# Every second column of a head per product, w_in loaded in column halves, v loaded in head halves

## The chip, the core and the metric

The kernel runs on one core of a Trainium2 chip. Its time is what one execution takes on the device, in microseconds. The times below are medians of several executions; beside them stands one execution taken by the hardware profiler, from which all lines of the profile come. In these lines PE is TensorE's matrix multiplication, PEld its weight load, DVE is VectorE, ACT is ScalarE, POOL is GpSimd, and SP is SyncE, which here only issues DMAs. A q behind an engine (POOLq, SPq) is its queue of instructions.

## What is computed

Attention with a forget gate, for 8 batches of 8 heads with 576 positions and a head width of 64, then a two-layer network with gelu over all heads together (4608 rows of 512, hidden width 2048):

```python
scores = scale * np.matmul(q, k.transpose(0, 1, 3, 2))
cum = np.cumsum(np.log(np.clip(f, 0.0001, 1.0)), axis=-1)
decay = cum[:, :, :, None] - cum[:, :, None, :]
scores = np.where(causal, -1000000000.0, scores + decay)
attn = softmax(scores)                         # cut: max, exp, sum
attn_out = np.matmul(attn, v)
x = attn_out.transpose(0, 2, 1, 3).reshape(B * S, H * D)
out = gelu_tanh(x @ w_in) @ w_out
```

## The kernel before

**Quads.** The heads are worked four at a time. Quad i holds four heads of batch i//2, so there are 16 quads and two of them make the 512 columns of x for one batch. For a quad, q and k are loaded by GpSimd's queue with a cast to bf16 (`load_qk`, L94) and transposed by VectorE (`transpose_qk`, L120). The decay is split: exp(−cum − 64) of a key's position, `wT`, is multiplied into v (`make_vw`, L129), so a product with the exponentials of the scores carries it; the factor of the query's position cancels when the product is divided by the denominator, which is the product of the same exponentials with `w_bf`, the bf16 copy of `wT`.

**Rounds.** A quad's scores are computed in three rounds (`score_round`, L139), each of which fills two pairs of PSUM banks; ScalarE writes their exponentials into the strips of `pt` (L166), and GpSimd sets what lies above the diagonal to zero (`mask(i, r)`, L169): two instructions for round 0, one for round 1, two for round 2.

**Products.** `product` (L186) adds six parts, the slots in `product_parts` (L183): the first four need the masks of rounds 0 and 1, the last two that of round 2. `denominators(i)` (L226) does it with `w_bf` into the bank pair "po", and VectorE turns the result into reciprocals spread over the partitions (`reciprocals`, L213: a transpose, L215, a reciprocal, L217, and a transpose back, L219). `attn_out(i, y)` (L229) does it with half y of the head's columns of `vw`, and `normalise` (L223) multiplies with the reciprocals and writes `xT[:, 2*(i%2)+y, :]`: 32 columns of four heads on 128 partitions. The pool of "po" has one buffer, so the next user of it waits until VectorE has read the last.

**The network.** `w_in_sb` (128, 4, 2048) holds w_in in the order of these partitions: for slab dt = 2u+y the rows of half u, column half y of each head. `mlp_in(b, fts)` (L249) goes over blocks of 128 hidden columns, four slabs each, and ScalarE applies gelu (L245). `mlp_out` (L260) multiplies with `w_out`; in the later steps its matmuls are dealt out between the rounds of the next quads (`step`, `pull`).

**Order.** Everything runs in the order in which it is written, on each engine (`manual_schedule`). Dependencies between instructions and the waits for them are worked out by the framework. GpSimd's queue carries all loads with a cast, the masks and, from quad 2 on, make_vw; so whatever is issued there stands ahead of what comes later.

**The start.** `startup` (L294) is written out by hand for quads 0 and 1. GpSimd issues q and k of quads 0 and 1, fills the unused part of `v_nat` with zeros (L299), issues the five loads of v for batch 0 (L102, one for each tile of 128 positions, all 8 heads in it) and slab 0 of w_in (L112); then come the masks of quad 0 with slabs 1 to 3 of w_in between them, the masks of quad 1, the q and k of quad 2 between mask(1,1) and mask(1,2), and the four loads of w_out (L116). VectorE does the scan of log f, the transposes of q and k, and make_vw(0) and make_vw(1). TensorE's order is: three score rounds of quad 0 and two of quad 1 with matmuls on a blank tile (`warm_up`, L290) between them, `denominators(0)`, the last score round of quad 1, `attn_out(0, 0)`, `attn_out(0, 1)`, then for quad 1 the first four parts of the denominators and of the product, their last two parts, the second product, and the first two column blocks of the network.

These are the two lines on which the order of w_in and of v rests:

```python
w_in_hbm = moe_w_in.rearrange("(u g y i) n -> u y g i n", u=QPB, g=4, y=2)
in_=v[b, :, s0:s0 + 128 - r, :].rearrange("h p d -> p h d")
```

Of the kernel before, what the change touches and what calls it, by code (L numbers as in the profile page):

```python
# [16 lines left out]
def kernel(  # L17
# [10 lines left out]
    nc = tc.nc  # L28

    B, H, S, D = q.shape  # L30
    BH = B * H
    NT = (S + 127) // 128
    LAST = S - 128 * (NT - 1)
    scale = 1.0 / (D ** 0.5)

    D_MODEL, D_FF = moe_w_in.shape
# [3 lines left out]
    QPB = H // 4  # L40
# [6 lines left out]
    TAIL, HEAD = NT - 1, NT  # L47
# [14 lines left out]
    def many(n, shape, dtype, name):  # L62
        return [singles.tile(shape, dtype, name=f"{name}{i}") for i in range(n)]
# [6 lines left out]
    v_nat = many(2, [128, NT, H, D], FP32, "v_nat")  # L70
# [3 lines left out]
    vw = many(2, [128, NT + 1, 4, D], BF16, "vw")  # L74
# [3 lines left out]
    w_in_sb = singles.tile([128, N_DT, D_FF], BF16, name="w_in_sb")  # L78
# [3 lines left out]
    wT = singles.tile([128, NQ, NT, 4], FP32, name="wT")  # L82
# [11 lines left out]
    def load_qk(i):  # L94
        b, h0 = i // QPB, 4 * (i % QPB)
        return [nc.gpsimd.dma_start(  # L96
            out=dst[i % 2].rearrange("p a d -> p (a d)"),
            in_=src[b, h0:h0 + 4].rearrange("h (p a) d -> (h p) (a d)", p=32))
            for src, dst in ((k, k_c), (q, q_c))]

    def load_v(b, eng=nc.sync):
        return [eng.dma_start(  # L102
            out=v_nat[b % 2][r:, t, :, :],
            in_=v[b, :, s0:s0 + 128 - r, :].rearrange("h p d -> p h d"),
        ) for t, r, s0 in [(t, 0, 128 * t) for t in range(TAIL)] + [(TAIL, 128 - LAST, S - LAST)]]


    w_in_hbm = moe_w_in.rearrange("(u g y i) n -> u y g i n", u=QPB, g=4, y=2)
    w_out_hbm = moe_w_out.rearrange("(t p) n -> p t n", p=128)

    def load_w_in(dt):
        nc.gpsimd.dma_start(out=w_in_sb[:, dt, :], in_=w_in_hbm[dt // 2, dt % 2])  # L112

    def load_w_out(c):
        n = N_FT // 4
        return nc.gpsimd.dma_start(out=w_out_sb[:, n * c:n * (c + 1), :],  # L116
                            in_=w_out_hbm[:, n * c:n * (c + 1), :])


    def transpose_qk(i):  # L120
        for src, dst in ((k_c, kT), (q_c, qT)):
            nc.vector.transpose(  # L122
                out=dst[i % 2].rearrange("p s c -> p (s c)").bitcast(FP32)
                    .rearrange("p (t a) -> p a t", a=S // 32),
                in_=src[i % 2].rearrange("p a d -> p (a d)").bitcast(FP32)
                    .rearrange("p (a d) -> p a d", d=D // 2),
            )

    def make_vw(i, eng=nc.gpsimd):  # L129
        h0 = 4 * (i % QPB)  # L130
        for p, n, slot in ((128, NT, 0), (64, 1, HEAD)):
            eng.tensor_mul(  # L132
                vw[i % 2][:p, slot:slot + n], v_nat[(i // QPB) % 2][:p, 0:n, h0:h0 + 4, :],
                wT[:p, i, 0:n, :].unsqueeze(3).to_broadcast([p, n, 4, D]))

    def bank_pair(tag, name):
        return pools[tag].tile([128, 2, 512], FP32, name=name, tag=tag)

    def score_round(i, r, tags=("s", "s")):  # L139
        off, parts = rounds[r]  # L140
        n = sum(x[2] for x in parts)
        tiles = [bank_pair(x, "ps_s") for x in tags]
        kk, qq, p = kT[i % 2], qT[i % 2], pt[i % 2]
        def block(c, m0, m, k0, q0, nq, c0, fresh):
            for h in range(4):
                nc.tensor.matmul(  # L146
                    tiles[h // 2][m0:m0 + m, h % 2, c0:c0 + nq],
                    kk[32 * h:32 * h + 32, k0:k0 + m, c],
                    qq[32 * h:32 * h + 32, q0:q0 + nq, c],
                    start=(c == 0 and fresh), stop=(c == 1),  # L150
                    skip_group_check=True,
                )

        if r == 0:
            for c in range(2):
                block(c, 0, 64, 0, 0, 512, 0, True)
                block(c, 64, 64, 64, 64, 448, 64, True)
                block(c, 64, 64, S - LAST, S - LAST, LAST, 0, False)
        else:
            c0 = 0  # L160
            for (t, q0, nq) in parts:
                for c in range(2):
                    block(c, 0, 128, 128 * t, q0, nq, c0, c0 == 0)
                c0 += nq
        for g in range(2):
            nc.scalar.activation(p[:, 2 * g:2 * g + 2, off:off + n],  # L166
                                 tiles[g][:, :, 0:n], AF.Exp, scale=scale)
# [58 lines left out]
    def denominators(i):  # L226
        reciprocals(i, product(i, den_groups(i), bank_pair("po", "po")))

    def attn_out(i, y, tag="po"):  # L229
        normalise(i, y, product(i, out_groups(i, y), bank_pair(tag, "po")))  # L230
# [52 lines left out]
    def make_w(cum):  # L283
        for (r, t0, t1) in ((0, 0, TAIL), (128 - LAST, TAIL, NT)):
            nc.scalar.activation(
                wT[r:, :, t0:t1, :].rearrange("p i t h -> p t i h"),
                cum[r:, t0 * BH:t1 * BH].rearrange("p (t i h) -> p t i h", i=NQ, h=4),
                AF.Exp, scale=-1.0, bias=shift[r:, :])

    def warm_up(ps, n):  # L290
        for _ in range(n):
            nc.tensor.matmul(ps[:, 0, :], blank[:, 0:128], blank, start=True, stop=True)  # L292

    def startup():  # L294
        nc.sync.dma_start(out=f_sb, in_=f.rearrange("b h s -> (b h) s"))
        load_qk(0)
        make_identity(nc, ident_f32)
        for t_ in v_nat:
            nc.gpsimd.memset(t_[:128 - LAST, TAIL, :, :], 0.0)  # L299
        load_qk(1)  # L300
        load_v(0, nc.gpsimd)
        load_w_in(0)

        nc.vector.memset(blank, 0.0)  # L304
        warm = bank_pair("po", "warm")
        warm_up(warm, 11)
        nc.vector.memset(ones_f32, 1.0)
        nc.vector.memset(shift, -64.0)
        nc.vector.memset(wT[:128 - LAST, :, TAIL, :], 0.0)
        nc.vector.memset(w_bf[LAST:, :, HEAD, :], 0.0)  # L310
        for t_ in vw:
            nc.vector.memset(t_[LAST:, HEAD, :, :], 0.0)
        nc.vector.tensor_scalar(f_sb, f_sb, 1e-4, 1.0, op0=ALU.max, op1=ALU.min)
        nc.scalar.activation(f_sb, f_sb, AF.Ln)
        nc.vector.tensor_tensor_scan(cum_sb, ones_f32, f_sb, 0.0, op0=ALU.mult, op1=ALU.add)
        cum = bank_pair("x", "small")[:, 0, 0:NT * BH]
        for t in range(NT):
            s0 = min(128 * t, S - 128)
            nc.tensor.transpose(cum[:, t * BH:(t + 1) * BH],
                                cum_sb[:, s0:s0 + 128], ident_f32)  # L320
        make_w(cum)
        warm_up(warm, 6)
        transpose_qk(0)
        transpose_qk(1)
        nc.vector.tensor_copy(w_bf[:, :, :NT, :], wT)
        nc.vector.tensor_copy(w_bf[:LAST, :, HEAD, :], wT[:LAST, :, 0, :])
        make_vw(0, nc.vector)
        make_vw(1, nc.vector)

        for r, tags in enumerate((("s", "s"), ("x", "s"), ("s", "x"))):  # L330
            score_round(0, r, tags)
            warm_up(warm, 5)
            mask(0, r)
            load_w_in(r + 1)
        score_round(1, 0)
        warm_up(warm, 5)
        score_round(1, 1, ("x", "s"))
        denominators(0)
        mask(1, 0)
        score_round(1, 2, ("s", "x"))  # L340
        attn_out(0, 0)
        mask(1, 1)
        load_qk(2)
        attn_out(0, 1, "s")
        mask(1, 2)
        for c in range(4):
            load_w_out(c)
        first, rest = slice(0, 4), slice(4, 6)
        pod, po0, po1 = (bank_pair(x, "po") for x in ("s", "po", "x"))
        product(1, den_groups(1), pod, first)  # L350
        product(1, out_groups(1, 0), po0, first)
        reciprocals(1, product(1, den_groups(1), pod, rest))
        r0 = product(1, out_groups(1, 0), po0, rest)
        r1 = product(1, out_groups(1, 1), po1)
        ph0, ph1 = (bank_pair("s", "ps_h") for _ in range(2))
        mlp_mm(0, 0, ph0, (0, 1))
        normalise(1, 0, r0)
        normalise(1, 1, r1)
        mlp_mm(0, 1, ph1, (0, 1))
        for dt in (2, 3):  # L360
            mlp_mm(0, 0, ph0, (dt,))
            mlp_mm(0, 1, ph1, (dt,))
        gelu(0, 0, ph0)
        gelu(0, 1, ph1)
        load_qk(3)
        after(load_v(2)[0], load_v(1, nc.gpsimd)[-1])
# [39 lines left out]
    with tc.manual_schedule():  # L406
# [5 lines left out]
        for b in range(B):  # L412
# [18 lines left out]
            elif b + 1 < B:  # L431
                i = 2 * b + 3
# [36 lines left out]
```

## Time and profile before

| | us |
|---|---|
| median of 3 executions (351.93 to 352.19) | 352.18 |
| the profiled execution | 351.2 |
| its span, first to last instruction | 349.5 |
| TensorE busy in it | 334.8 |

The mean granted clock of TensorE over the span is 0.989 of full speed. The span begins with the first instruction; the profiled execution has 1.7 us around it. The views used below are: the chain of work that ended last, in order of time (start, length, engine, tile and line, count); the timeline (start, length, engine, line, operation, output and inputs, count, and in brackets the idle time before it with what ended it); windows (for a stretch of time: its length, busy time and count of each engine in the order PE, PEld, DVE, ACT, POOL, then the granted clock, the share of the DMA engines' time and GB/s); groups by line (busy time, mean ns of one, idle time before them); and issues of DMAs (count, KB as written, median us from issue to landing).

### The profile page before, as it was taken

What the parts mean: (1) busy time and instruction counts of PE and PEld (TensorE: products, weight loads), DVE (VectorE), ACT (ScalarE), POOL (GpSimd) and SP (SyncE); (2) the same over time, 40 slices, a digit from 0 to 9 for tenths busy, and PEclk for the clock granted to TensorE, in tenths of its full rate; (3) what the DMA queues carried; (4) which work ended last, traced back from release to release, by engine and by line L of the source; (5) the groups of instructions that cost most, each with busy time, mean ns of one, the idle gap of its engine ahead of it and who ended that gap; (6) DMA issues with size and microseconds to landing.
All of it is one profiled execution on the core that took longest, in us unless ns stands there. A gap on an engine that the chain in (4) does not pass through costs nothing.

```text
span 349.5 us, 10980 instructions
## 1 busy us (share of the span) xinstructions
PE 334.8 (96%) x5022; PEld 197.5 (57%) x5022; DVE 122.1 (35%) x163; ACT 198.1 (57%) x244; POOL 125.6 (36%) x166
## 2 busy tenths in 40 slices
PE   6938999999999999999999999999999999999995
PEld 2425754467544774457544675457644675557642
DVE  6477032743244503424234422425143312430021
ACT  4851666776655566656745567565664566515400
POOL 8784219765143242625044251624026400300000
PEclk9978999999999999999999999999999999999999
DMA  7999998349510490109511292117301000010021
GB/s 133 190 181 188 218 197 203 64 80 231 100 64 34 118 209 7 62 33 199 103 57 42 69 212 53 35 62 168 68 34 62 33 32 2 33 64 30 2 86 64
DMA packets 43007, 33.37 MB, mean 95 GB/s; under 512 B 31056, under 2 KB 33104, under 8 KB 42960
## 3 DMA queue, kind: packets, MB, share of 16 engines
q0 software_dynamic: 9568, 16.00, 25.8%
q1 hardware_dynamic: 33392, 16.67, 17.3%
q8 instruction: 39, 0.64, 0.8%
q14 instruction: 8, 0.07, 0.1%
HBM read 36.85 MB, written 9.44 MB: 132 GB/s over the span
## 4 chain that ended last, share of the span: by engine, by line
PE 86%; ACT 3%; DMA 3%; DVE 2%; issue 2%; POOL 2%; ACTq 0%; DVEq 0%; POOLq 0%
PE ps_h L236 36%; PE pso L268 32%; PE po L193 10%; PE ps_s L146 8%; DMA v_nat<-in_v_dram 3%; ACT pt L166 3%; DVE vw L132 1%; POOL v_nat L102 1%; DVE den L215 0%; POOL q_c L96 0%; POOL k_c L96 0%; POOL v_nat L299 0%; DVE rb L219 0%; DVE xT L224 0%; DVE o_st L273 0%
## 5 line engine op out<-in xcount | busy, mean ns | idle before, releaser
L268 PE MATMUL pso<-w_out_sb,gT 128*32 128x512 bf16 (+1 forms) x1908 | 134.6, 379 | 0.0
L236 PE MATMUL ps_h<-xT,w_in_sb 128*128 128x288 bf16 x1024 | 128.6, 286 | 1.2 <-ACT gT L245 0.5
L245 ACT ACTIVATE gT<-ps_h 128x576 bf16<-128x576 f32 x128 | 82.3, 650 | 72.3 <-PE ps_h L236 72.3
L166 ACT ACTIVATE pt<-ps_s 128x1024 bf16<-128x1024 f32 x96 | 92.5, 1025 | 48.6 <-PE ps_s L146 47.8
L236 PEld LDWEIGHTS <-w_in_sb 128*128 128x128 bf16 x1024 | 99.3, 98 | 31.5 <-issue 4.7
L177 POOL TENSOR_SCALAR_AFFINE_SELECT pt<-pt 128x512 bf16<-128x512 bf16 (+1 forms) x80 | 52.1, 659 | 130.7 <-ACT pt L166 129.4
L268 PEld LDWEIGHTS <-gT 128*32 128x32 bf16 (+1 forms) x1908 | 59.1, 97 | 53.2 <-issue 0.8
L273 DVE COPY o_st<-pso 128x512 f32<-128x512 f32 x36 | 24.7, 685 | 70.3 <-PE pso L268 70.2
L215 DVE STREAM_TRANSPOSE den<-po 128x576 f32<-128x576 f32 x16 | 12.5, 782 | 83.7 <-PE po L193 83.7
L132 POOL TENSOR_TENSOR vw<-v_nat,wT 128x1280 bf16<-128x1280 f32 (+1 forms) x28 | 40.6, 1472 | 0.2
L224 DVE TENSOR_TENSOR xT<-po,rb 128x576 bf16<-128x576 f32 x32 | 24.1, 757 | 46.3 <-PE po L193 46.2
L146 PE MATMUL ps_s<-qT,kT 32*64 32x64 bf16 (+6 forms) x896 | 36.2, 293 | 1.6 <-ACT pt L166 0.7
L193 PE MATMUL po<-pt,vw 128*32 128x64 bf16 (+4 forms) x768 | 29.1, 289 | 5.3 <-DVE den L215 5.3
L146 PEld LDWEIGHTS <-kT 32*128 32x128 bf16 (+1 forms) x896 | 15.3, 98 | 27.4 <-issue 24.0
L193 PEld LDWEIGHTS <-vw 128*32 128x32 bf16 x768 | 13.9, 100 | 20.0 <-issue 11.2
L122 DVE STREAM_TRANSPOSE kT<-k_c 128x576 f32<-128x576 f32 x16 | 19.9, 1245 | 12.4 <-DMA k_c<-in_k_dram 12.4
L122 DVE STREAM_TRANSPOSE qT<-q_c 128x576 f32<-128x576 f32 x16 | 19.9, 1243 | 1.3 <-DMA q_c<-in_q_dram 1.1
L96 POOL DMA_DIRECT2D k_c<-in_k_dram x16 | 9.1, 572 | 29.2 <-DVE kT L122 24.8
L193 PE MATMUL po<-pt,w_bf 128*32 128x512 bf16 (+5 forms) x384 | 14.7, 285 | 0.0
L219 DVE STREAM_TRANSPOSE rb<-rec 128x576 f32<-128x576 f32 x16 | 12.4, 778 | 0.5
L166 ACT ACT_TABLE_LOAD x7 | 9.0, 1283 | 5.9 <-PE ps_s L146 5.9
L292 PE MATMUL warm<-blank 128*128 128x512 bf16 x37 | 10.4, 427 | 1.3 <-DVE blank L304 1.3
(32 smaller groups left out, 62.9 us busy)
## 6 DMA issues: line engine op xcount, KB each, us to landing
out_dram<-o_st SPq DMA_DIRECT2D x36, 256.0 KB, 2.0
v_nat<-in_v_dram SPq DMA_DIRECT2D x24, 256.0 KB, 6.2
k_c<-in_k_dram POOLq DMA_DIRECT2D x16, 288.0 KB, 6.0
q_c<-in_q_dram POOLq DMA_DIRECT2D x16, 288.0 KB, 7.0
v_nat<-in_v_dram POOLq DMA_DIRECT2D x8, 256.0 KB, 10.8
w_in_sb<-in_moe_w_in_dram POOLq DMA_DIRECT2D x4, 512.0 KB, 16.3
w_out_sb<-in_moe_w_out_dram POOLq DMA_DIRECT2D x4, 512.0 KB, 14.2
v_nat<-in_v_dram SPq DMA_DIRECT2D x6, 128.0 KB, 8.8
```

The source lines that it names most:

```text
L122: nc.vector.transpose(out=dst[i % 2].rearrange("p s c -> p (s c)").bitcast(FP32) .rearrange("p (t a) -> p a t", a=S // 32), in_=src[i % 2] ...
L132: eng.tensor_mul(vw[i % 2][:p, slot:slot + n], v_nat[(i // QPB) % 2][:p, 0:n, h0:h0 + 4, :], wT[:p, i, 0:n, :].unsqueeze(3).to_broadcast([ ...
L146: nc.tensor.matmul(tiles[h // 2][m0:m0 + m, h % 2, c0:c0 + nq], kk[32 * h:32 * h + 32, k0:k0 + m, c], qq[32 * h:32 * h + 32, q0:q0 + nq, c ...
L166: nc.scalar.activation(p[:, 2 * g:2 * g + 2, off:off + n], tiles[g][:, :, 0:n], AF.Exp, scale=scale)
L177: nc.gpsimd.affine_select(out=p[p0:p1, :, o:o + 128], in_=p[p0:p1, :, o:o + 128], compare_op=ALU.is_ge, fill=0.0, base=0, pattern=pattern, ...
L193: nc.tensor.matmul(po[r0:r0 + w.shape[-1], o:o + nq], w, p[:, h, col:col + nq], start=(n < 2), stop=(n in (0, len(product_parts) - 1)), sk ...
L215: nc.vector.transpose(out=den, in_=po)
L224: nc.vector.tensor_mul(xT[i // QPB % 2][:, 2 * (i % QPB) + y, :], po, rbs[i])
L236: nc.tensor.matmul(ph[:, j, 0:hS], w_in_sb[:, dt, 128 * ft:128 * ft + 128], xT[b % 2][:, dt, hS * j:hS * (j + 1)], start=(dt == 0), stop=( ...
L245: nc.scalar.activation(gT[:, ft, o:o + S].rearrange("p (j n) -> p j n", j=2), ph[:, :, 0:hS], AF.Gelu_apprx_tanh)
L268: nc.tensor.matmul(ps[m:m + w, :], gT[:, ft, c + m:c + m + w], w_out_sb[:, ft, :], start=(ft == 0), stop=(ft == N_FT - 1), skip_group_chec ...
L273: nc.vector.tensor_copy(st, ps)
```

## The change

- The two products of a quad take the even and the odd columns of each head instead of the lower and the upper 32. `make_vw` writes each half with an instruction of its own that reads every second column of v, so it has four instructions instead of two; `vw` then holds the even columns ahead of the odd ones.
- So slab 2u+y of w_in is made of the rows 256u + 2p + y: partition p holds two neighbouring rows. A load takes both of them for 1024 of the 2048 columns, and there are two such loads for a column half. All slabs of the first half are loaded where slab 0 was, those of the second half between mask(0,0) and mask(0,1), where slab 1 was; the loads after mask(0,1) and mask(0,2) are gone.
- v of batch 0 is loaded in ten loads, first heads 0 to 3 of every tile, then heads 4 to 7. Later batches load as before.
- The zeros of `v_nat` are written by VectorE, ahead of its work on f, instead of by GpSimd.

```diff
-    def load_v(b, eng=nc.sync):
+    def load_v(b, eng=nc.sync, heads=slice(0, H)):
         return [eng.dma_start(
-            out=v_nat[b % 2][r:, t, :, :],
-            in_=v[b, :, s0:s0 + 128 - r, :].rearrange("h p d -> p h d"),
+            out=v_nat[b % 2][r:, t, heads, :],
+            in_=v[b, heads, s0:s0 + 128 - r, :].rearrange("h p d -> p h d"),
         ) for t, r, s0 in [(t, 0, 128 * t) for t in range(TAIL)] + [(TAIL, 128 - LAST, S - LAST)]]
...
-    w_in_hbm = moe_w_in.rearrange("(u g y i) n -> u y g i n", u=QPB, g=4, y=2)
+    w_in_hbm = moe_w_in.rearrange("(u p y) n -> u p y n", u=QPB, y=2)
...
-    def load_w_in(dt):
-        nc.gpsimd.dma_start(out=w_in_sb[:, dt, :], in_=w_in_hbm[dt // 2, dt % 2])
+    def load_w_in(c):
+        n = slice(D_FF // 2 * c, D_FF // 2 * (c + 1))
+        for u in range(QPB):
+            nc.gpsimd.dma_start(out=w_in_sb[:, 2 * u:2 * u + 2, n], in_=w_in_hbm[u, :, :, n])
...
         for p, n, slot in ((128, NT, 0), (64, 1, HEAD)):
-            eng.tensor_mul(
-                vw[i % 2][:p, slot:slot + n], v_nat[(i // QPB) % 2][:p, 0:n, h0:h0 + 4, :],
-                wT[:p, i, 0:n, :].unsqueeze(3).to_broadcast([p, n, 4, D]))
+            for y in range(2):
+                eng.tensor_mul(
+                    vw[i % 2][:p, slot:slot + n, :, 32 * y:32 * y + 32],
+                    v_nat[(i // QPB) % 2][:p, 0:n, h0:h0 + 4, y::2],
+                    wT[:p, i, 0:n, :].unsqueeze(3).to_broadcast([p, n, 4, D // 2]))
...
         make_identity(nc, ident_f32)
-        for t_ in v_nat:
-            nc.gpsimd.memset(t_[:128 - LAST, TAIL, :, :], 0.0)
         load_qk(1)
-        load_v(0, nc.gpsimd)
+        load_v(0, nc.gpsimd, slice(0, 4))
+        load_v(0, nc.gpsimd, slice(4, 8))
         load_w_in(0)
...
         for t_ in vw:
             nc.vector.memset(t_[LAST:, HEAD, :, :], 0.0)
+        for t_ in v_nat:
+            nc.vector.memset(t_[:128 - LAST, TAIL, :, :], 0.0)
...
             mask(0, r)
-            load_w_in(r + 1)
+            if r == 0:
+                load_w_in(1)
```

## The prediction

> **What bounds the kernel now.** I read the page first, for the busy time by engine.
>
> ```profile
> PE 334.8 (96%) x5022; PEld 197.5 (57%) x5022; DVE 122.1 (35%) x163; ACT 198.1 (57%) x244; POOL 125.6 (36%) x166
> ```
>
> TensorE is busy for 96% of the span and the change takes no matmul away, so only what TensorE waits for can be won. Next, the chain in order of time (start, length, what):
>
> ```profile
> 4.99 3.51 POOL v_nat L102 x4
> 8.50 10.24 DMA v_nat<-in_v_dram
> ...
> 18.82 4.43 DVE vw L132 x4
> 23.25 0.70 DVE den L215
> ...
> 23.99 4.68 PE po L193 x77
> ...
> 28.70 0.80 DVE den L215
> ...
> 33.32 13.88 PE ps_h L236 x112
> ```
>
> Up to 18.8 us the end hangs on the five loads of v; then the four multiplications of make_vw on VectorE, then the transpose of the first denominators (queued behind them), and only at 23.99 TensorE. From 33.32 on the chain is TensorE almost without a break (the last row: 14 blocks of columns at 0.99). So the change is worth what it moves in the first 33 us. The timeline shows what the queues do there:
>
> ```profile
> 18.09 0.63 PE L146 MATMUL ps_s<-qT,kT 32*128 32x320 bf16 x14 [0.16 <-ACT pt L166]
> 23.99 2.86 PE L193 MATMUL po<-pt,vw 128*32 128x64 bf16 x48 [5.28 <-DVE den L215]
> 4.97 4.26 POOL L102 DMA_DIRECT2D v_nat<-in_v_dram  x5
> 11.70 1.34 POOL L177 TENSOR_SCALAR_AFFINE_SELECT pt<-pt 64x512 bf16<-64x512 bf16 x2 [1.76 <-ACT pt L166]
> 9.68 11.11 ACT L166 ACTIVATE pt<-ps_s 128x1024 bf16<-128x1024 f32 x12 [1.85 <-PE ps_s L146]
> 15.37 1.22 POOL L177 TENSOR_SCALAR_AFFINE_SELECT pt<-pt 128x512 bf16<-128x512 bf16 x2 [0.31 <-ACT pt L166]
> 19.08 1.72 POOL L177 TENSOR_SCALAR_AFFINE_SELECT pt<-pt 128x512 bf16<-128x512 bf16 x1 [0.47 <-ACT pt L166]
> 25.80 0.74 POOL L116 DMA_DIRECT2D w_out_sb<-in_moe_w_out_dram  x1 [0.56 <-DMA w_in_sb<-in_moe_w_in_dram]
> 30.44 0.74 POOL L116 DMA_DIRECT2D w_out_sb<-in_moe_w_out_dram  x1 [3.90 <-DMA w_in_sb<-in_moe_w_in_dram]
> ```
>
> Two things are to be seen. Two strips are masked in 1.22 us, but one takes 1.72 while make_vw runs on VectorE: the two take turns. And GpSimd waits for old loads before it issues new ones. The times from issue to landing (rows of short windows, each holding one issue: q at 4.44, v's tiles 0, 2 and 4 at 4.97, 6.75 and 8.50, w_in at 9.18) tell which:
>
> ```profile
> q_c<-in_q_dram POOLq DMA_DIRECT2D x1, 288.0 KB, 6.5
> v_nat<-in_v_dram POOLq DMA_DIRECT2D x1, 256.0 KB, 7.1
> v_nat<-in_v_dram POOLq DMA_DIRECT2D x1, 256.0 KB, 7.8
> v_nat<-in_v_dram POOLq DMA_DIRECT2D x1, 128.0 KB, 10.2
> w_in_sb<-in_moe_w_in_dram POOLq DMA_DIRECT2D x1, 512.0 KB, 16.3
> 11.00:14.60 3.60, 3.60 (x44) 1.54 (x42) 2.09 (x3) 3.60 (x5) 2.79 (x5) 1.00 1.08 211
> 14.60:18.70 4.10, 3.94 (x85) 1.58 (x69) 0.00 (x0) 4.10 (x5) 3.63 (x6) 1.00 0.94 123
> ```
>
> w_in's first load lands at 9.18+16.3 = 25.5, and the w_out issue that waits for it starts at 25.80; counted over GpSimd's issues it is the eighth after it. The next w_out waits in the same way for w_in's second load. So an issue on GpSimd waits for the eighth before it to land. Landings are 10.9 (second q), 12.1, 14.6 and 18.7 (v): 1.25 us a tile at first, then the rate drops from 211 to 123 GB/s (last column of the window rows) once w_in's loads are in the queue.
>
> **The change part by part.** The sum is made against the profiled execution: span 349.5, 351.2 us in all, 1.0 under the median of 352.18. I carry the difference over.
>
> *v in halves.* Each half holds half the 256-byte pieces, so I take half the pitch: 0.62 us a half tile. The first four heads land at 10.9 + 4.5×0.62 = 13.7, the rest at 16.5 if the drop does not come back. make_vw(0), which needs only the first, starts at 13.75 instead of 18.82.
>
> *Issues.* The rows:
>
> ```profile
> L96 POOL DMA_DIRECT2D k_c<-in_k_dram x16 | 9.1, 572 | 29.2 <-DVE kT L122 24.8 <-DMA w_out_sb<-in_moe_w_out_dram 2.1 <-DMA q_c<-in_q_dram 1.5
> L116 POOL DMA_DIRECT2D w_out_sb<-in_moe_w_out_dram x4 | 3.0, 758 | 4.5 <-DMA w_in_sb<-in_moe_w_in_dram 4.5
> L299 POOL MEMSET v_nat<- 64x512 f32 x2 | 1.0, 514 | 0.0
> 3.67 0.58 DVE L313 TENSOR_SCALAR f_sb<-f_sb 64x576 f32<-64x576 f32 x1 [1.35 <-DMA f_sb<-in_f_dram]
> ```
>
> The removed memsets give GpSimd back 0.9 of their 1.0 us, so v starts at 4.05. On VectorE they lie, at about the same length, in the 1.35 us wait for f; without that cover they would cost their 1.0. A half issue costs between k's 0.57 and whole v's 0.85 (4.26/5); I take w_out's 0.76, which also has four pieces a partition. Ten halves and two w_in loads then stand ahead of the first mask, each from the ninth issue on behind a landing: the third half of the second group waits for q's 10.9, the first w_in for half tile 2 (12.8), the second for half tile 3 (13.4). They are out at 14.45, while the first mask used to start at 11.70. **This is the price of the change**: the masks of quad 0 are late by over 2 us. At 0.85 an issue it would be 0.4 more; at 0.57 the landings still pace the queue.
>
> *make_vw.* Its rows (VectorE at the start, GpSimd later):
>
> ```profile
> L132 DVE TENSOR_TENSOR vw<-v_nat,wT x4: 842/1161/1492, 18.8 to 22.4; 128x1280 bf16<-128x1280 f32 x2, 64x256 bf16<-64x256 f32 x2
> L132 POOL TENSOR_TENSOR vw<-v_nat,wT 128x1280 bf16<-128x1280 f32 x14 | 32.7, 2335 | 0.2
> L132 POOL TENSOR_TENSOR vw<-v_nat,wT 64x256 bf16<-64x256 f32 x14 | 8.5, 610 | 0.0
> ```
>
> On VectorE the large one takes 1.4 from start to start; halves are 0.74, the small ones 0.2 (their 0.84 was mostly waiting for a mask). No row shows a VectorE multiplication that reads every second fp32, so the bound is 0.74 to 1.44 a half; I take 0.74, since each element is still one step of the instruction, and keep the other as a rival. [...] On GpSimd the line through 2335 and 610 gives 0.18 + 1.685 ns an element, so four halves take 3.3 instead of 2.95: 0.37 more.
>
> *Taking turns.* VectorE's multiplications and the masked strips alternate, 0.64 a strip. The first half of make_vw(0) runs to 14.5, a strip of mask(0,0) to 15.2, the second half to 15.9, the second strip to 16.5. w_in's second column half is issued in two times 0.68, by 17.9; meanwhile VectorE does the small ones, and from 16.8 the two halves of make_vw(1), to 18.4. Then mask(0,1) to 19.1, and the two strips of mask(0,2) with a small multiplication of 0.23 ahead of each, to 20.0 and 20.9 (15.37+1.22 = 16.59 before). VectorE is through with both make_vw at 20.2 (23.25 before). So **the mask takes the wait over from vw**: the first denominators' last parts end on TensorE 0.3 after it, at 21.2, and their transpose starts there instead of at 23.25. The last score round of quad 1 is queued behind them on TensorE: 0.7 for it and 1.9 for its two exponentials (11.11/12 each) give 23.8 instead of 20.8 (9.68+11.11). GpSimd does three more strips to 22.8, the next k and q issues to 23.9, and mask(1,2) to 25.2.
>
> *TensorE from there.* The clock decides:
>
> ```profile
> 20.00:22.00 2.00, 0.00 (x0) 0.09 (x1) 2.00 (x3) 1.98 (x2) 2.00 (x4) 0.81 1.07 190
> 22.00:24.00 2.00, 0.01 (x3) 0.01 (x3) 1.97 (x4) 0.09 (x1) 2.00 (x3) 0.50 1.03 207
> ```
>
> The mean of 0.81 puts the fall to half at 21.2, 2.5 us after the last matmul (18.72). In the changed kernel TensorE has two pauses of about 1.5 us with little between them, so I take one stretch at half clock. Products start at 22.0; the two of quad 0 take 2.86 (the row at 23.99, at half clock); 32 matmuls for the first parts of quad 1's denominators and product take 2.86/48×32/2 = 0.95 at full clock; the rest 0.3, with mask(1,2) just done, and gaps 0.1: the second denominators are ready at 26.2 instead of 28.70. What follows (transpose, reciprocal, two normalisations, then w_in's matmuls) is unchanged. **Gain 2.5**; at full clock mask(1,2) limits at 25.5: 3.2.
>
> *w_in.* It is read from about 27 on. Behind v's 16.5, a column half of 1.05 MB at 198 GB/s (20 to 24 us) takes 5.3: 21.8 and 27.1, the second not needed before 33.32−2.5+6×0.99 = 36.8. Hidden by 5 us; if v's drop returned, by 2.5.
>
> *Later.* The second quad pair is the next narrow place:
>
> ```profile
> v_nat<-in_v_dram POOLq DMA_DIRECT2D x1, 128.0 KB, 9.3
> 53.48 2.90 POOL L132 TENSOR_TENSOR vw<-v_nat,wT 128x1280 bf16<-128x1280 f32 x2
> 57.40 1.22 POOL L177 TENSOR_SCALAR_AFFINE_SELECT pt<-pt 128x512 bf16<-128x512 bf16 x2 [0.43 <-ACT pt L166]
> ```
>
> v of batch 1, issued at 42.55, lands at 51.85; make_vw(2) would start at 51.0, and the loads have gained about 4.1×(1−123/211) = 1.7, so it is there. The 0.37 more fits into the 0.43 for which the mask waited. Beyond that GpSimd idles between masks. Nothing is given back.
>
> The sum: 349.5 − 2.5 = 347.0 of span, **349.7** beside the median.
>
> **The rivals.** (1) *The drop returns* (14%): the second heads land at 18.75, VectorE is through at 23.0, gain 0.65: 351.5. For it: nothing in the trace names the cause. Against: it begins when w_in's loads join. [...]
> (2) *Part is given back at 51 us* (12%): if v of batch 1 lands no earlier than 51.85, make_vw(2) is 0.85 late, plus 0.37, less 0.43: 350.5.
> (3) *The halves do not free make_vw* (8%): the change does not do what it says if the multiplication waits for the whole tile. Then both make_vw fall among the masks, VectorE ends at 24.3: 0.6 slower, 352.8. Against: ScalarE's twelve exponentials run in one piece from 9.68 while masks of the same tile wait between them, so parts of a tile are told apart.
> (4) *A half load takes as long as a whole one* (9%), the slower side: 1.25 us each, the landings hold GpSimd's queue and with it the masks; the second heads land at 22.2, mask(1,2) at 28.7: 2.8 lost, 355.0. It decides from about 0.92 us a half. For it: tiles 3 and 4, one and a half tiles of pieces, took 4.1 together (14.6 to 18.7). Against: they fell into the drop. [...]
> (5) *Reading every second element costs double* (7%): 0.7 lost at the start; on GpSimd 2.95 more before mask(2,1), 0.43 hidden, so TensorE waits some 2.5 at 58: 355.4.
>
> **How the numbers follow.** Forecast 50%, its own range 349.0 (full clock) to 350.2 (dearer issues). All else is as above. The range leaves out (4) and (5) and reaches from 348.4 (full clock, and loads sooner by half a microsecond) to 352.9, which takes in (1) to (3). A measurement can tell about 0.2%, 0.7 us: faster is under 351.5. Faster: 50 + 12 + half of (1) = 69%; within: 7 + 5 of (3) = 12%; slower: 9 + 7 + 3 = 19%.
>
> **What would show it.** Right: make_vw starts near 13.8, the first mask near 14.5 behind a w_in issue, mask(0,2) ends near 20.9, the first denominators' transpose starts near 21.2 and the second's near 26; w_in is waited for nowhere. Wrong: make_vw still released at 16 or later; two multiplications of 1.4 us; TensorE waiting for a mask near 55. The prediction fails most easily in GpSimd's queue, where every landing delays all masks behind it.

## The result, and the profile after

The changed kernel takes **348.96 us** (median of 4, 348.55 to 349.31), beside 352.19 for the kernel before (median of 4, 351.93 to 352.40): a ratio of **0.9908, 95% interval 0.9891 to 0.9925**. Some executions of the kernel before run at a lower mean clock and take over 1.5% longer (357.4 us at 0.979, say); the ratios here and below leave them out. The profiled execution took 348.87, with a span of 347.2: 2.3 less than the 349.5 before, where the forecast had 2.5. The medians are 3.2 apart, because the profiled execution of before lay 1.0 under its median and that of the changed kernel 0.1.

The page's busy times after (rows as in the prediction's first fence):

```profile
PE 334.9 (96%) x5022; PEld 197.6 (57%) x5022; DVE 124.6 (36%) x169; ACT 198.4 (57%) x244; POOL 131.5 (38%) x197
```

TensorE does the same work. What changed is when it starts. The chain of work that ended last, in order of time:

```profile
9.84 5.59 ACT pt L171 x6
...
15.50 1.17 POOL pt L182
16.67 1.37 POOL w_in_sb L115 x2
...
18.10 2.71 POOL pt L182 x3
...
20.86 0.28 PE po L198 x4
...
21.16 0.79 DVE den L220
...
22.00 4.39 PE po L198 x88
...
26.41 0.80 DVE den L220
...
31.02 13.88 PE ps_h L241 x112
```

Before, this chain ran through the loads of v to 18.82 and make_vw to 23.25. Now v and make_vw are gone from it. GpSimd's queue stands in their place: a mask, the two loads of w_in's second half, and three more masks. The row that was at 33.32 is at 31.02, which is the whole 2.3 us. The timeline has the single pieces:

```profile
13.39 1.41 POOL L115 DMA_DIRECT2D w_in_sb<-in_moe_w_in_dram  x2
13.99 3.01 DVE L136 TENSOR_TENSOR vw<-v_nat,wT 128x640 bf16<-128x640 f32 x4 [1.19 <-DMA v_nat<-in_v_dram]
14.81 1.86 POOL L182 TENSOR_SCALAR_AFFINE_SELECT pt<-pt 64x512 bf16<-64x512 bf16 x2
17.68 3.27 DVE L136 TENSOR_TENSOR vw<-v_nat,wT 128x640 bf16<-128x640 f32 x4 [0.67 <-DMA v_nat<-in_v_dram]
18.10 4.77 POOL L182 TENSOR_SCALAR_AFFINE_SELECT pt<-pt 128x512 bf16<-128x512 bf16 x6
22.00 2.84 PE L198 MATMUL po<-pt,vw 128*32 128x64 bf16 x48 [0.32 <-DVE den L220]
23.92 1.23 POOL L182 TENSOR_SCALAR_AFFINE_SELECT pt<-pt 128x512 bf16<-128x512 bf16 x2
```

make_vw(0) starts at 13.99, make_vw(1) at 17.68 behind a landing of v, and VectorE is through with both at 20.95, 0.2 before the denominators' transpose. Three window rows follow (columns as in the prediction's rows: engines, then clock, DMA share, GB/s):

```profile
14.60:18.70 4.10, 2.81 (x57) 1.12 (x55) 3.43 (x6) 4.10 (x5) 3.98 (x6) 1.00 1.00 128
22.00:24.00 2.00, 2.00 (x40) 1.27 (x43) 1.48 (x3) 1.98 (x3) 1.93 (x5) 0.52 1.13 213
24.00:26.00 2.00, 2.00 (x51) 1.16 (x44) 1.06 (x2) 0.95 (x1) 2.00 (x4) 0.63 1.12 210
```

The last two show the half clock that was forecast: their means of 0.52 and 0.63 put it from 22.1 to 25.5. The first is a warning. In the window in which the rate had fallen to 123 GB/s before, it is 128 now. So the drop, whose return was the prediction's rival (1), is there again, and the time came all the same. That is where the experiments begin. One more row is needed below, the page's group of make_vw on GpSimd (busy time, mean ns of one, idle time before):

```profile
L136 POOL TENSOR_TENSOR vw<-v_nat,wT 128x640 bf16<-128x640 f32 (+1 forms) x56 | 44.9, 830 | 0.2
```

### The profile page after: what moved, and what is told of

Read it like the earlier page. It is cut to its first block, busy times and chain, and to the rows that moved or that the text cites. A ratio compares the mean times of both kernels' runs of the same rounds, so it can differ in the third digit from the quotient of the medians.

```text
span 347.2 us, 11023 instructions
## 1 busy us (share of the span) xinstructions
PE 334.9 (96%) x5022; PEld 197.6 (57%) x5022; DVE 124.6 (36%) x169; ACT 198.4 (57%) x244; POOL 131.5 (38%) x197
## 4 chain that ended last, share of the span: by engine, by line
PE 87%; ACT 5%; issue 2%; DMA 2%; POOL 2%; DVE 2%; ACTq 0%; DVEq 0%; POOLq 0%
PE ps_h L241 36%; PE pso L273 32%; PE po L198 10%; PE ps_s L151 8%; ACT pt L171 5%; DMA q_c<-in_q_dram 2%; POOL pt L182 1%; DVE den L220 0%; POOL w_in_sb L115 0%; DVE qT L125 0%; DVE rb L224 0%; DVE xT L229 0%; DVE o_st L278 0%; ACT gT L250 0%; POOL k_c L96 0%
## 5 line engine op out<-in xcount | busy, mean ns | idle before, releaser
L171 ACT ACTIVATE pt<-ps_s 128x1024 bf16<-128x1024 f32 x96 | 92.6, 1024 | 51.7 <-PE ps_s L151 51.6
L136 POOL TENSOR_TENSOR vw<-v_nat,wT 128x640 bf16<-128x640 f32 (+1 forms) x56 | 44.9, 830 | 0.2
L151 PEld LDWEIGHTS <-kT 32*128 32x128 bf16 (+1 forms) x896 | 15.1, 97 | 27.4 <-issue 23.9
L102 POOL DMA_DIRECT2D v_nat<-in_v_dram x15 | 11.5, 775 | 8.2 <-DMA w_out_sb<-in_moe_w_out_dram 5.0
L198 PEld LDWEIGHTS <-w_bf 128*1 128x1 bf16 (+1 forms) x384 | 6.5, 89 | 10.6 <-issue 6.1
```

What stands on the lines that cost most here:

```text
L136: eng.tensor_mul(vw[i % 2][:p, slot:slot + n, :, 32 * y:32 * y + 32], v_nat[(i // QPB) % 2][:p, 0:n, h0:h0 + 4, y::2], wT[:p, i, 0:n, :].u ...
L151: nc.tensor.matmul(tiles[h // 2][m0:m0 + m, h % 2, c0:c0 + nq], kk[32 * h:32 * h + 32, k0:k0 + m, c], qq[32 * h:32 * h + 32, q0:q0 + nq, c ...
L171: nc.scalar.activation(p[:, 2 * g:2 * g + 2, off:off + n], tiles[g][:, :, 0:n], AF.Exp, scale=scale)
L198: nc.tensor.matmul(po[r0:r0 + w.shape[-1], o:o + nq], w, p[:, h, col:col + nq], start=(n < 2), stop=(n in (0, len(product_parts) - 1)), sk ...
```

## The experiments

The theory that came from the prediction: the halves of v free make_vw(0) early, and w_in's spread over 128 partitions only keeps v's rate up. The rival: the old w_in loads were what held v, so the spread alone gives the gain and the halves matter little. Each run below was timed in five rounds against the kernel before on the same chip; a span is that of the run's profiled execution. Lines of a kernel made from the one before are numbered as there, give or take two.

### Without the halves: whole_v

From the changed kernel, v of batch 0 in five whole loads.

```diff
-        load_v(0, nc.gpsimd, slice(0, 4))
-        load_v(0, nc.gpsimd, slice(4, 8))
+        load_v(0, nc.gpsimd)
```

> The changed kernel with v of batch 0 in five whole loads again; all else as changed. If the halves are what frees make_vw (my theory): the masks of quad 0 are on time again (mask(0,2) ends near 16.6), but make_vw starts only when all of v is there, 16.6 to 18.7, and VectorE is through with both at about 23.5: 351.3 to 352.4. If the gain is that of w_in's new order (rival): 349.0 as changed.

350.07 us, ratio 0.9944 (0.9918 to 0.9969), span 347.6. Its chain:

```profile
7.72 8.18 DMA v_nat<-in_v_dram
...
15.98 4.96 DVE vw L136 x8
20.95 0.70 DVE den L220
...
21.70 5.12 PE po L198 x83
...
26.84 0.80 DVE den L220
...
31.47 8.61 PE ps_h L241 x69
```

The chain is again that of before, v, make_vw, denominators, but all of it earlier: v is complete at 15.90 instead of 18.74, and the first denominators' transpose starts at 20.95, even 0.2 ahead of the changed kernel. The last row is 0.45 behind the changed kernel's 31.02. Two window rows show where the lead was lost:

```profile
20.00:22.00 2.00, 0.30 (x8) 0.19 (x11) 1.93 (x6) 1.86 (x2) 1.93 (x4) 0.53 1.13 213
24.00:26.00 2.00, 2.00 (x44) 1.15 (x40) 0.79 (x2) 0.00 (x0) 2.00 (x4) 0.50 1.11 213
```

TensorE's clock is at half from 20.1 and still at 26, where the changed kernel's had come back at 25.5, so the products up to the second denominators take 5.12 us here and 4.39 there. The lead went to the clock and not to the loads. My theory had this kernel at 351.3 or more and the rival at 349.0: the time lies between, 1.2 below the one and 1.1 above the other. The profiled span has kept 1.9 of the 2.3, but this execution was the fastest of the twelve (349.35).

### The spread alone: spread_only

From the kernel before: the products take every second column, and each of the four w_in loads writes a slab over all 128 partitions in one sweep, partition p holding row 256u + 2p + y. The places of the loads and v stay as they were.

```diff
-    w_in_hbm = moe_w_in.rearrange("(u g y i) n -> u y g i n", u=QPB, g=4, y=2)
+    w_in_hbm = moe_w_in.rearrange("(u p y) n -> u y p n", u=QPB, y=2)
...
+            for y in range(2):
...
+                    v_nat[(i // QPB) % 2][:p, 0:n, h0:h0 + 4, y::2],
```

> The kernel before with only the even and odd columns and w_in's four slabs over 128 partitions of every second row, at their old places; v in whole tiles. If w_in's spread over few engines causes the drop in rate while v lands: v is there by 16.6, make_vw starts 2 us sooner: 350.3. If it does not (the drop is also in the trace of the changed kernel, 121 to 157 GB/s from 14 to 20 us): v lands near 18.7 and the divided make_vw costs 0.3 to 0.5 on VectorE: 352.5.

350.12 us where 350.3 was expected of the theory, ratio 0.9936 (0.9908 to 0.9963), span 347.5 in the fastest of the twelve executions. The window in which the rate fell before:

```profile
14.60:18.70 4.10, 3.73 (x78) 1.44 (x61) 2.29 (x3) 4.10 (x6) 3.38 (x5) 1.00 1.06 208
```

And two pieces of its chain:

```profile
16.41 5.17 DVE vw L133 x8
21.58 0.70 DVE den L217
```

With the loads at the same places and of the same size, the rate is 208 GB/s instead of 123, and make_vw starts at 16.41 instead of 18.82. **The layout of w_in was the cause of the drop**: the only other edit, the divided make_vw, comes behind v. Why the old layout is slow is not shown, since the trace has the rate and the DMA engines' mean share but not the engine of each packet. In halves_only below, which keeps the old layout, that share is 0.28 from 16 to 18 us, the time of 4.5 of the 16 engines, at 49 GB/s, with the last of v and one slab, later two, in the queue; here it is 1.05 in the same window, at 213 GB/s. In the prediction the drop was only a rival's condition; the layout is the main source of the gain.

### The halves alone: halves_only

From the kernel before, only the ten half loads of v.

```diff
-        load_v(0, nc.gpsimd)
+        load_v(0, nc.gpsimd, slice(0, 4))
+        load_v(0, nc.gpsimd, slice(4, 8))
```

> The kernel before with only v of batch 0 in head halves; w_in in four slabs behind the masks, zeros on GpSimd, make_vw undivided. Theory: make_vw starts near 14 and the first products near 22 here too, but w_in's fourth slab, issued behind mask(0,2) at about 20.5, lands near 31 and TensorE waits for it before its first column blocks: 350.3 to 351.3. If w_in's order has no part in the gain: 349.0. If the halves have none: 352.2.

**356.84 us, ratio 1.0129 (1.0083 to 1.0174)**, span 356.0: 4.5 slower by the ratio, where my theory wanted it faster. First a window row:

```profile
18.00:20.00 2.00, 0.36 (x4) 0.09 (x4) 1.89 (x2) 1.16 (x2) 1.99 (x3) 1.00 0.53 72
```

Then TensorE's timeline:

```profile
30.72 0.91 PE L236 MATMUL ps_h<-xT,w_in_sb 128*128 128x288 bf16 x6 [3.21 <-DMA w_in_sb<-in_moe_w_in_dram]
34.24 1.14 PE L236 MATMUL ps_h<-xT,w_in_sb 128*128 128x288 bf16 x4 [2.61 <-DMA w_in_sb<-in_moe_w_in_dram]
36.16 1.14 PE L236 MATMUL ps_h<-xT,w_in_sb 128*128 128x288 bf16 x4 [0.78 <-DMA w_in_sb<-in_moe_w_in_dram]
```

And the piece of the chain that ends with the last of these waits:

```profile
20.86 15.26 DMA w_in_sb<-in_moe_w_in_dram
```

The halves do what they were meant to do: make_vw starts at 14.13 and the products at 22.09. But the ten issues push w_in's first load from 9.18 to 13.48 and the last from 16.54 to 20.86. In the window row v is complete (at 17.98) and only slabs are in the queue, three of them: the DMA engines are busy for 0.53 of their time and move 72 GB/s, where spread_only has 1.08 and 215 in the same window. So the slabs land from 26.95 to 36.11, and TensorE waits for three of them: its long run in the network starts at 37.56 instead of 33.32, and its 112 matmuls take 16.11 us instead of 13.88, the first 11 of them 2.80 at half clock. What was a background load became the bound. On the old layout the half loads only lose.

### w_in behind the masks: w_in_later

From the changed kernel, w_in's first half behind mask(0,0) and the second behind mask(0,2), to take the price that the prediction named (masks late by over 2 us) away from the first masks.

```diff
-        load_w_in(0)
...
-            if r == 0:
-                load_w_in(1)
+            if r != 1:
+                load_w_in(r // 2)
```

> The changed kernel with w_in's first column half issued behind mask(0,0) and its second behind mask(0,2), instead of ahead of mask(0,0) and of mask(0,1). If GpSimd's queue now sets the end (theory): mask(0,2) ends near 19.5 instead of 20.8, then VectorE's make_vw(1) is the next bound at about 20.3, gain 0.5 to 0.8 on the changed kernel: 348.3. If w_in becomes late by it (rival): its first half lands near 26 and TensorE waits: 349 to 350. If w_in's loads cause v's drop, v's second half lands near 16 here instead of 17.6.

349.64 us, ratio 0.9922 (0.9892 to 0.9952), span 348.1: no gain over the changed kernel. Its chain from 24 us on:

```profile
24.83 1.23 POOL pt L182 x2
26.06 1.45 POOL w_out_sb L119 x2
...
41.15 11.20 DMA v_nat<-in_v_dram
...
52.51 3.20 POOL vw L136 x4
```

The clock does not fall here (0.999 over the execution; the products take 1.55 instead of 2.84), and still nothing is gained: mask(0,2) ends at 20.30, 0.5 earlier than in the changed kernel (19.5 was expected), but mask(1,2) ends at 26.06 instead of 25.15, because the two w_in issues only moved to another place in the same queue. And w_in being later, everything behind it is: v of batch 1 lands at 52.35 and holds make_vw(2), which is the prediction's rival (2). The time is where this run's rival had it, but not by its mechanism: w_in's first half lands at 22.68 and 25.19 and is not waited for. Moving the issues within GpSimd's queue did not take the price away.

The expectation had a second question, whether w_in's loads hold v. The last half tile lands at 17.27 here (17.55 in the changed kernel), though the first w_in load is issued only at 15.83. So the second heads are as late with hardly anything of w_in in the queue.

### The half clock: keep_clock

From the changed kernel, seven matmuls on the blank tile ahead of `denominators(0)`, into its banks, to fill TensorE's pauses before the products.

```diff
-        denominators(0)
+        po = bank_pair("po", "po")
+        warm_up(po, 7)
+        reciprocals(0, product(0, den_groups(0), po))
```

> The changed kernel with seven blank matmuls ahead of the first denominators, so that TensorE's pauses before 22 us are short (they add work whose result is thrown away). If the fall to half clock costs what the prediction said: the two products of quad 0 take 1.55 instead of 2.84, and mask(1,2), done at 25.2, is the next bound: the second denominators at 25.5 instead of 26.4, 0.9 less than the changed kernel. If GpSimd's queue sets the end regardless of the clock (rival): no change.

**347.82 us, ratio 0.9868 (0.9839 to 0.9897)**, span 346.6. TensorE's timeline:

```profile
21.68 1.55 PE L198 MATMUL po<-pt,vw 128*32 128x64 bf16 x48 [0.32 <-DVE den L220]
24.84 0.25 PE L198 MATMUL po<-pt,w_bf 128*1 128x192 bf16 x4 [0.28 <-POOL pt L182]
```

And its chain further on:

```profile
39.32 11.52 DMA v_nat<-in_v_dram
...
51.01 3.20 POOL vw L136 x4
```

The products of quad 0 take 1.55 instead of 2.84: the half clock had cost 1.3 us there. Then mask(1,2) limits at once (the wait in the second row), as the prediction said for full clock, and the second denominators are transposed at 25.15 (25.5 expected). The network's long run starts at 29.76, 1.26 earlier than in the changed kernel, but only 0.6 of it reaches the end. v of batch 1 lands at 50.84 as it did there (50.55), and now that the masks before it are done earlier, make_vw(2) waits 1.17 us for it.

### Four slabs instead of column halves: slabs_halves

From the kernel before: v in halves as in halves_only, slabs over 128 partitions as in spread_only. So it is the changed kernel without its column halves, with one slab behind each mask of quad 0 and the zeros of `v_nat` on GpSimd.

```diff
+    w_in_hbm = moe_w_in.rearrange("(u p y) n -> u y p n", u=QPB, y=2)
...
+            for y in range(2):
...
-        load_v(0, nc.gpsimd)
+        load_v(0, nc.gpsimd, slice(0, 4))
+        load_v(0, nc.gpsimd, slice(4, 8))
```

> Head halves of v, even and odd columns, and w_in over 128 partitions, but in four slabs behind the masks as before instead of in column halves; zeros on GpSimd as before. If w_in's spread over the partitions is what the halves of v need (theory): its last slab, issued near 21, lands near 29, in time: same as the changed kernel within 0.3. If the column halves are needed (rival): TensorE waits for the last slab, 1 us or more slower than the changed kernel.

348.70 us, ratio 0.9890 (0.9856 to 0.9923), span 345.7: not to be told from the changed kernel. Its chain is through GpSimd's queue as well:

```profile
23.34 1.25 POOL pt L179 x2
24.64 0.28 PE po L195 x4
24.95 0.79 DVE den L217
```

The column halves have no measurable part in the gain. Spread and v halves together carry it. Beside spread_only this kernel differs in the half loads of v alone, and its second denominators come at 24.95 instead of 26.70 and its span is 345.7 instead of 347.5 (each the fastest execution of its kernel; the medians are 1.4 apart, on two chips, and the intervals of the ratios overlap).

### make_vw(1) later: vw1_after

If v is complete at 15.9 anyway, the four multiplications of make_vw(1) need not stand ahead of the first denominators. From whole_v, they go behind `reciprocals(0)` on VectorE.

```diff
-        make_vw(1, nc.vector)
...
         denominators(0)
+        make_vw(1, nc.vector)
```

> The changed kernel with v in whole loads, and make_vw(1) behind the reciprocals of quad 0 on VectorE. w_in's issues then stand early and v lands near 16; make_vw(0) ends near 18.5, the first denominators are transposed there, products from about 19.4 without a fall of the clock, the second denominators near 24.0 instead of 26.4: 2.4 less than the changed kernel, 346.6 beside a median of 352.2. If GpSimd's masks of quad 1 or make_vw(2) near 49 us (v of batch 1 lands near 47.8) become the bound (rival): 1 less at most.

348.62 us where 346.6 was expected, ratio 0.9889 (0.9859 to 0.9920), span 346.5. TensorE's timeline:

```profile
20.33 2.86 PE L198 MATMUL po<-pt,vw 128*32 128x64 bf16 x48 [1.85 <-DVE den L220]
22.95 0.77 PE L198 MATMUL po<-pt,w_bf 128*32 128x64 bf16 x16
24.81 0.65 PE L198 MATMUL po<-pt,vw 128*32 128x64 bf16 x16 [1.09 <-DVE xT L229]
```

v lands at 16.65. The products come 1.7 earlier than in the changed kernel, but after a pause of 1.85 they run at half clock (0.50 from 20 to 22 us), and then TensorE waits 1.09 for VectorE, where make_vw(1) lies ahead of the normalisation that frees the bank pair "po". The long run starts at 30.35, 0.7 ahead of the changed kernel's. One wait went, and the half clock and the next engine's queue took most of what it was worth.

### The zeros back on GpSimd: memset_back

From the changed kernel, the two memsets of `v_nat` on GpSimd, where they were before.

```diff
+        for t_ in v_nat:
+            nc.gpsimd.memset(t_[:128 - LAST, TAIL, :, :], 0.0)
```

> The changed kernel with the zeros of v_nat on GpSimd again, 1 us ahead of its loads. Theory: from the tenth issue on GpSimd waits for landings, which the DMA engines pace and not the issue; so at most 0.3 slower than the changed kernel. Rival: the whole queue moves, 0.9 slower.

348.46 us, ratio 0.9883 (0.9853 to 0.9914), span 346.3: not slower. Its chain:

```profile
11.23 2.11 POOL v_nat L102 x3
13.34 1.41 POOL w_in_sb L115 x2
```

w_in's first issue starts at 13.33, beside 13.39 in the changed kernel. In both, the last three half loads are issued only when q of quad 1 is there (landed at 10.95 here and at 11.02 there), and w_in's issues follow them without a break. So that one landing holds the queue, and from there on it is the length of the issues, not further landings as the theory had it. Moving the zeros had no measurable part in the gain.

### v of batch 1 first: v1_first

From keep_clock, to test what gave 0.6 us back: v of batch 1 ahead of q and k of quad 3, whose transposes move one round later.

```diff
-        load_qk(3)
-        after(load_v(2)[0], load_v(1, nc.gpsimd)[-1])
+        load_v(1, nc.gpsimd)
+        after(load_v(2)[0], load_qk(3)[-1])
...
-            if (i, r) in ((2, 0), (3, 1)):
+            if (i, r) in ((2, 1), (3, 1)):
```

> The kernel with the seven blank matmuls (keep_clock, span 346.6) with v of batch 1 loaded ahead of q and k of quad 3, whose transposes move from the first to the second round of quad 2. My theory: from 20 to 51 us the loads share a full queue and land in the order of issue, so v of batch 1 (landed at 50.84 there, 1.1 us after the two masks of quad 2's first round were done) lands two loads of 1.4 us earlier, near 48; make_vw(2) then starts behind the masks at 49.9, and the 0.6 us that were given back at 56 us come back: span 346.0, 0.6 under that kernel. Rival: the wait only moves to q and k of quad 3, which then land near 51.5 and are transposed by 54, after the scores of quad 3 are wanted (53.5): within 0.2 of 346.6 or slower.

347.38 us, span 345.6. The ratio is 0.9822 (0.9785 to 0.9860), but on this chip the kernel before ran at 353.92 and scattered from 351.92 to 360.28, so I compare the spans. GpSimd's timeline:

```profile
48.19 1.36 POOL L182 TENSOR_SCALAR_AFFINE_SELECT pt<-pt 64x512 bf16<-64x512 bf16 x2 [3.93 <-ACT pt L171]
49.63 3.22 POOL L136 TENSOR_TENSOR vw<-v_nat,wT 128x640 bf16<-128x640 f32 x4
```

v of batch 1 lands at 47.62 instead of 50.84, and make_vw(2) starts behind the masks without a wait. The span is 1.0 less than keep_clock's: 0.3 was there already at the start of the long run (29.47 beside 29.76), and the other 0.7 comes behind it, where 0.6 had been given back. The wait is gone from the trace, so v of batch 1 was its cause. The size is less sure: keep_clock's profiled execution was one of its two slowest, and the medians are only 0.4 apart, on two chips.

### The masks first: masks_first

From slabs_halves, the edits of keep_clock and v1_first, and q and k of quad 2 behind mask(1,2) instead of ahead of it.

```diff
         mask(1, 1)
-        load_qk(2)
         attn_out(0, 1, "s")
         mask(1, 2)
+        load_qk(2)
```

> The kernel with slabs over 128 partitions and v in halves (slabs_halves, span 345.7, second denominators' transpose at 24.95 right behind mask(1,2)), with three edits for the waits that are left: the loads of q and k of quad 2 go behind mask(1,2), seven blank matmuls hold the clock, and v of batch 1 goes ahead of q and k of quad 3. If GpSimd's queue is the bound of the start, as the prediction says, mask(1,2) ends near 23.5, TensorE is the next bound, the second denominators are transposed at 24.2, 0.75 earlier, and the span is 345.0. Rival: something else holds the start (the reciprocals of quad 0 on VectorE, or the half clock in spite of the blank matmuls): second denominators not before 24.8, span 345.5 or more.

347.41 us, ratio 0.9824 (0.9777 to 0.9870; beside the same scattered times of the kernel before), span 345.9. The rival was right, as the chain shows:

```profile
19.10 2.38 DVE vw L133 x4
21.48 0.70 DVE den L217
22.23 2.87 PE po L195 x88
25.12 0.80 DVE den L217
```

And TensorE's row of the products:

```profile
22.23 1.55 PE L195 MATMUL po<-pt,vw 128*32 128x64 bf16 x48 [1.93 <-DVE den L217]
```

mask(1,2) is done by 23.9 and the clock holds through a pause of 1.93 us (1.00 from 20 to 24), yet the second denominators come at 25.12 rather than the 24.2 I expected. make_vw started 0.44 later than in slabs_halves, and VectorE's eight multiplications took 7.25 us instead of 6.05: make_vw(0)'s two small ones, of which the shortest in the changed kernel takes 0.27, took 2.61 (16.49 to 19.10) around two masked strips (17.62 to 18.85). So make_vw on VectorE, between masks, sets the start here. The spans of its six runs go from 344.9 to 347.2; that the two engines' turns fall differently each time may be the reason, but one trace does not show it.

The two last kernels are at about 347.4 us and keep_clock at 347.82, beside 348.96 for the changed kernel; these were different sessions and chips, with 352.36 to 353.92 for the kernel before. On keep_clock's own chip memset_back, which is the changed kernel but for the zeros, took 348.46, so the seven blank matmuls are worth some 0.6 us there by the medians.

## Why the prediction was right, and where it was not

The time was right: 349.7 forecast, 348.96 measured, 2.3 us between the profiled spans for 2.5. That the median moved by 3.2 is the 1.0 that was carried over from the kernel before, whose profiled execution lay that far under its median; the changed kernel's lay 0.1 under, so the carried term was 0.9 too large.

**Right, step by step.** make_vw starts at 13.99 (13.75 forecast). The issues end at 14.80 (14.45) and the first mask starts behind them, as the price said. VectorE is through with make_vw at 20.95 (20.2). The last mask of quad 0 ends at 20.82 (20.9); the first denominators' transpose starts at 21.16 (21.2), the products at 22.00 (22.0), in 2.84 at half clock (2.86). mask(1,2) ends at 25.15 (25.2), the second transpose starts at 26.41 (26.2). w_in is waited for nowhere: its halves are complete at 23.88 and 28.86, some 2 later than forecast (21.8 and 27.1), its first matmul is at 27.19, and what was forecast as hidden stays hidden. A multiplication that reads every second column costs 0.74 from start to start on VectorE, and four halves 4×830 ns = 3.3 us on GpSimd, as reckoned; rival (5) is out. make_vw(0) starts 3.5 before the other heads have landed, so rival (3) is out. The first four half tiles land 0.57 to 0.76 apart, not 1.25, so rival (4) is out. In the changed kernel nothing is given back later.

**Right, with some luck: the half clock.** It was forecast as one stretch from two pauses of about 1.5 us. The pauses were 1.64 and 0.81, the clock fell at 22.1, as the products began, and was back at 25.5. The mean clock differs between executions of one kernel: two of the four have 0.990 (349.31 and 349.04 us) where the others have 0.993 and 0.994, and they are the slower two.

**Wrong: the part that got the credit.** The step "make_vw(0), which needs only the first, starts at 13.75 instead of 18.82" put the gain on the halves. But 18.82 was itself made by w_in's old layout. With the new layout and whole loads of v, make_vw starts at 16.41 (spread_only) or 15.98 (whole_v), and the ratios are 0.9936 and 0.9944: some six tenths of the gain without any half load. The halves move make_vw another 2 us ahead but put ten issues in front of the masks. What that leaves is not settled. Between whole_v and the changed kernel it is 0.4 in the spans, and the first denominators come at 20.95 without the halves and at 21.16 with them; between spread_only and slabs_halves it is 1.8, and they come at 21.58 without and at 20.14 with. In the ratios it is 0.36% and 0.46%, with intervals that overlap.

**Wrong in the same step: a change of two parts was weighed as one.** Half loads on the old layout lose 1.3%. The prediction's "hidden by 5 us" for w_in is true of the new layout alone.

**Mis-sized: when the second heads land.** 16.5 was forecast if the drop did not come back, which was the author's assumption; they landed at 17.55, and the rate in 14.6 to 18.7 was 128 GB/s. Of the 1.7 us that the loads were to have gained by 51 us, v of batch 1 showed 1.3: it landed at 50.55 for 51.85. By the prediction's rival (1) a drop costs nearly all of the gain. It cost nothing, since VectorE was through at 20.95 and the masks set the end. Rival (1) was mispriced because it took 18.75 for the landing. The rate of the window and this landing do not go together either: memset_back, keep_clock and v1_first have 123 to 131 GB/s in it, and their second heads land at 16.15 to 16.65.

**Right for another reason: the end of the issues.** The prediction let w_in's two issues wait for half tiles 2 and 3. These had landed at 12.86 and 13.62, and the issues at 13.39 and 14.09 followed those ahead of them without a pause: 0.70 to 0.75 each from q's landing at 11.02 on, 0.63 for the small last tile.

**The rival that came true elsewhere.** (2), v of batch 1 too late at 51 us, does not bite in the changed kernel, with 0.55 us in hand (landed at 50.55, the masks before it done at 51.10). It bites as soon as the start gets 1.26 faster, and v1_first shows it as the cause.

**Open.** Why the rate is low from 14.6 to 18.7 where half loads of v and column halves of w_in come together: 128 GB/s in the changed kernel and 123 to 131 in keep_clock, memset_back and v1_first. With half loads and slabs it is 179 (slabs_halves, masks_first), with whole loads of v and column halves 211 and 199 (whole_v, vw1_after). In the changed kernel the DMA share is 1.00 meanwhile, so the engines are not short of work; each KB takes them longer, 0.125 us against 0.086 in whole_v (a share of 1.00 of 16 engines' time for 128 GB/s, 1.14 for 211). What makes it longer was not tried. Nor do the medians settle what the halves are worth.

## What to carry to other kernels

When a load's rate falls, look at the shape of the other load that joined the queue: re-laying that background load gave most of this gain (123 to 208 GB/s, some six tenths by the ratios), and the visible half of the change, alone, lost 1.3%. Before crediting one part of a change, ask what the "instead of" number would be if only the other part were made. And a gain at the start is kept only as far as the next load's landing allows (0.6 of 1.26 us in keep_clock), so read that landing and the slack ahead of it before hoping for more.

## What the runs showed of the hardware

- A slab of w_in whose source goes over 128 rows in one dimension is also cheaper to issue than one in four groups of 32 rows, 512 KB each: 0.55 to 0.61 us in spread_only, 0.68 to 0.75 in the old layout.
- TensorE's clock can fall after short pauses, but the length of a pause does not decide it. One of 1.85 us in vw1_after, 1.84 in memset_back and 1.94 in slabs_halves went with a fall to half (0.50 from 20 to 22 us in all three); in the changed kernel two of 1.64 and 0.81 with 0.4 us of matmuls between them did (0.52 from 22 to 24). One of 1.93 in masks_first, with seven blank matmuls shortly before it, did not, nor two of 0.81 and 0.86 in w_in_later, nor the 0.52 of keep_clock (1.00 from 16 to 26 in these three).
- TensorE's stretch at half clock was not equally long in all runs. By the windows' granted clocks it goes from 22.07 to 25.48 in the changed kernel, 3.41 us, and from 22.3 to 25.7 in spread_only and 19.4 to 22.8 in slabs_halves, about the same; in the kernel before it goes from 21.2 to 28.1, twice as long, and in whole_v from 20.1 to past 26. Between whole_v and the changed kernel that makes 0.73 us in the products up to the second denominators (5.12 and 4.39), so an estimate is that one profiled execution can lie some tenths off another by the length of this stretch.
- VectorE's multiplications of make_vw and GpSimd's masks take turns, and how they fall costs time: from the first start to the last end the same eight multiplications took 4.96 us in whole_v, 6.05 in slabs_halves and 7.25 in masks_first, and a small one 0.27 at the shortest in the changed kernel, while two together took 2.61 in masks_first.
